# A tenth of a softmax's exponentials moved from ScalarE to VectorE, and the score banks of PSUM split 3+2+1

## The chip, the core and the metric

The kernel runs on one core of a Trainium2 chip. Its engines work side by side, each through its own queue in order: TensorE (PE in the profile; PEld is its weight load), VectorE (DVE), ScalarE (ACT), GpSimd (POOL), and SyncE (SP), which issues the DMAs. TensorE writes its results into PSUM, which has eight banks of 128 partitions by 512 fp32 numbers; VectorE and ScalarE read them from there. The metric is the time of one execution on the device in microseconds (us), the median of several.

## The reference

One token sequence of 2048 rows and 512 columns goes through a layer normalisation, and its result through two branches that are added to the input:

```python
xn = layernorm(x)                                  # 2048 x 512
q, k, v = split(xn @ wqkv)                         # 32 heads of 16
p = softmax(q @ k.T * 16**-0.5)                    # per head 2048 x 2048
A = (p @ v).reshape(2048, 512) @ wo
B = (relu(xn @ W_gate) * (xn @ W_up)) @ W_down     # 1792 wide
out = x + A + B                                    # bf16
```

The softmax needs 32 x 2048 x 2048 exponentials. With a head size of only 16, they are far more work than the matmuls per head would suggest.

## The kernel before

**Tiles.** Scores are computed transposed: a score tile is 128 keys by 512 queries of one head, fp32, one PSUM bank. There are 2048 of them, in the order of the list `tiles` (line 554): block of queries `c4` (4), group of heads `gg` (4), half `ee` (2), key tile `kt` (16), head `j` of four (the four heads sit in four strips of 32 partitions). Three tiles at a time make a unit (`UNIT = 3`, lines 555 and 751), 683 units in all, the last with two tiles. For each unit TensorE writes three score tiles into one half of `ps_sc` (six banks: two halves of three; line 765), ScalarE reads the three banks with one instruction, takes exp(x/4) and writes bf16 into a `ring` of 13 units (line 777). For each four tiles of one key tile TensorE multiplies the exponentials by `v_aug` (four small matmuls in four column strips, line 737) and accumulates over the 16 key tiles in bank 0 of `ps_b`. `v_aug` has a column of ones beside the 16 of v, so the sum of the exponentials comes along as a 17th row.

**After 16 key tiles** `normalise` (line 703) has VectorE copy bank 0 to `o_sb`, sends the row sums through two small DMAs with a reciprocal on VectorE between them, brings them back spread over the partitions (`rb`), and GpSimd multiplies (line 723).

**Everything else goes into bank 1 of `ps_b`**, the only free bank: the projections q and k, the gated branch (`glu`, line 593: four matmuls for `up`, a VectorE copy, four for `gate`, and a VectorE instruction for relu times up, line 612), and the output rows (`out_rows`, line 623: 14 matmuls with `Wd` and 8 with `Wo_p`, and an addition on VectorE). This work is cut into pairs of matmuls; a plan (lines 665 to 698) gives each pair a unit at which it is due.

**What sets the order.** The kernel records its operations with a duration each (`G.op`), and a planner (`Graph.run`) puts them into one fixed queue per engine by these durations, by priorities and by which buffers come free. Score matmuls have the best priority, and the exponentials' multiplication with v comes `PV_LAG` units later. `Graph.emit` then writes the queues with semaphore waits. On the chip nothing is reordered: an instruction that waits holds up all that stands behind it on its engine.

**Fillers.** In a unit in which no pair is due (from unit 25 on), TensorE runs two matmuls of zeros into the score bank ahead of the scores (line 763); their result is overwritten. There are 418 such matmuls.

Of the kernel before, what the change touches and what calls it, by code (L numbers as in the profile page):

```python
# [7 lines left out]
I32 = mybir.dt.int32  # L8
ACTF = mybir.ActivationFunctionType
# [16 lines left out]
UNIT = 3  # L26
NRING = 13
PV_LAG = 4.0
NWS = 4
NUP = 2  # L30
# [26 lines left out]
class Graph:  # L57
# [10 lines left out]
    def op(self, eng, dur, fn, reads=(), writes=(), prio=0.0, order=(), name="", stream=None, lat=None, after=None):  # L68
# [13 lines left out]
        for t in writes:  # L82
# [21 lines left out]
    def run(self):  # L104
# [46 lines left out]
        while n < len(ops):  # L151
# [18 lines left out]
            for t in o.acq:  # L170
                i = slot_for(t)[1]
                c = t.pool.cur[i]
                if c is not None:
                    for u in c.w + c.r:
                        if u.eng == e and e != "SP":
# [121 lines left out]
def bass_parallel_sum__mha_block__glu_gated_reglu__prompt_kernel(  # L297
# [14 lines left out]
    with ExitStack() as es:  # L312
# [24 lines left out]
        qT = sb("qT", [128, 6, 512], BF16)  # L337
        v_aug = sb("v_aug", [128, NT, H, VW], BF16)
        ring = sb("ring", [128, NRING * UNIT, 512], BF16)
# [6 lines left out]
        oT2 = sb("oT2", [128, 6, 512], BF16)  # L346
# [6 lines left out]
        P_b = Pool("b", 2)  # L353
        P_ring = Pool("ring", NRING)
        P_xn = Pool("xn", 4)
        P_q = Pool("q", 6)
# [5 lines left out]
        P_oT = Pool("oT", 14)  # L362
# [78 lines left out]
        def ln_block(b, pr):  # L441
# [24 lines left out]
            for i in range(4):  # L466
# [8 lines left out]
                elif i % 2 == 0:  # L475
                    tp = Tile("tp", P_b, [0, 1] if b < 3 else [1])
# [57 lines left out]
        def proj_k(gg, b, prio=0.0, tile=None, sub=0, slots=None, gap=0.02):  # L534
            t = tile or Tile("pk", P_b, [0, 1] if (gg, b) in ((0, 1), (0, 2)) else [1])
# [19 lines left out]
        units = [tiles[i:i + UNIT] for i in range(0, len(tiles), UNIT)]  # L555
        NU = len(units)

        def upos(c4, gg=0, ee=0, kt=0):
            return (((c4 * NGG + gg) * 2 + ee) * NT + kt) * 4 / UNIT
# [18 lines left out]
        for kt in range(NT):  # L578
            proj_v(kt, -684 + 10 * (kt // 4) + 0.1 * kt, allowed=(0, 1) if kt < 8 else (1,))


# [144 lines left out]
        def pv_group(key, kt, u):  # L726
# [6 lines left out]
            def pv(e):  # L733
                ins = None
                for j in range(4):
                    tr, i = src[j]
                    ins = e.matmul(ps_b[32 * j:32 * j + VN, 0, :], v_aug[:, kt, 8 * gg + 2 * j + ee, 0:VN],  # L737
                                   ring[:, UNIT * tr.slot + i, :], start=(kt == 0), stop=(kt == NT - 1), tile_position=(0, 32 * j))
                return ins
            rd = [t_vones, t_v[kt]]  # L740
            for tr, i in src:
# [8 lines left out]
        li = 0  # L750
        for u, cl in enumerate(units):
# [3 lines left out]
            ts = Tile("s%d" % u, P_sc)  # L755
            n = len(cl)

            def sc(e, ts=ts, cl=cl, idle=u > 24 and u not in busy):
                ins = None
                if idle:  # L760

                    for _ in range(2):
                        e.matmul(ps_sc[:, 3 * ts.slot, :], zeros[:, 0:128], zeros[:], start=True, stop=True)  # L763
# [56 lines left out]
```

## Time and profile before

| what | value |
| --- | --- |
| median of 3 runs | 969.16 us (968.02 to 971.45) |
| the profiled execution | 971.93 us, of which the span of its instructions 970.0 us |
| busy ACT | 925.9 us, 95% |
| busy PE | 804.9 us, 83% |
| busy DVE | 192.6 us, 20% |
| busy POOL | 54.0 us, 6% |
| DMA | 34.64 MB moved |
| granted TensorE clock, mean | 0.98 of full speed |

Lines such as L777 are lines of the kernel before. In the views by group, a row has the line, the engine, the operation, what it writes and reads, shapes and count; then busy time in us and the mean duration of one in ns; then the engine's idle time just ahead of them and what ended it. In the views by order of time, a row has its start in us from the start of the span and its length; equal instructions that follow each other are merged, so that a length can cover several. A duration in the profile runs from an instruction's start to its end. Instructions of one engine overlap there, since the next one starts while the last is draining; so the step from one to the next is shorter than the duration, and it is the step that counts when an engine is full.

### The profile page before, as it was taken

The page shows a single profiled execution, that of the slowest core. Times are in us where ns is not written, and L with a number is a line of the kernel's source. Part 1 is how long each engine was busy: PE and PEld are TensorE (multiplying, and loading weights), DVE is VectorE, ACT ScalarE, POOL GpSimd, SP SyncE. Part 2 cuts the span into 40 slices and gives each one's busy share as a digit, 9 for nine tenths or more (in the row PEclk, how much of TensorE's full clock was granted, in tenths as well). Part 3 has the DMA queues.
Part 4 walks back from the last instruction along what each step waited for, and adds up shares of the span by engine and source line. Part 5 has one row for each costly group of instructions (what it writes and reads, how often), then busy time and mean ns, then how long its engine had stood idle before and what let it go on. Part 6 is the DMA issues. An engine that isn't in the chain of part 4 may idle for free.

```text
span 970.0 us, 12635 instructions
## 1 busy us (share of the span) xinstructions
PE 804.9 (83%) x5482; PEld 205.6 (21%) x5584; DVE 192.6 (20%) x323; ACT 925.9 (95%) x690; POOL 54.0 (6%) x56
## 2 busy tenths in 40 slices
PE   7798888888888888888888888888888888888883
PEld 2222222222222222222222222222222222222220
DVE  7733122221000021111100111121100002221021
ACT  4699999999999999999999999999999999999992
POOL 3200000000000000000000000000000000000000
PEclk8899999999999999999999999999999999999996
DMA  5014011110000121111000011111100112210000
GB/s 159 16 41 108 18 33 34 34 34 12 2 28 29 39 50 29 23 39 45 12 23 23 26 30 46 45 45 30 26 2 23 35 34 70 57 40 22 23 13 33
DMA packets 84087, 34.64 MB, mean 36 GB/s; under 512 B 69952, under 2 KB 79936, under 8 KB 84032
## 3 DMA queue, kind: packets, MB, share of 16 engines
q1 hardware_dynamic: 84032, 33.83, 13.5%
q8 instruction: 44, 0.72, 0.3%
q14 instruction: 11, 0.09, 0.0%
HBM read 31.20 MB, written 2.36 MB: 35 GB/s over the span
## 4 chain that ended last, share of the span: by engine, by line
ACT 82%; PE 12%; DVE 3%; DMA 1%; issue 1%; SPq 0%; POOLq 0%; ACTq 0%
ACT ring L777 82%; PE ps_b L518 4%; PE ps_sc L763 3%; PE ps_sc L765 3%; PE ps_b L737 2%; DVE kT L542 1%; DMA x_sb<-in_A_x_dram 1%; DVE xn_sb L469 1%; DMA rb<-rec_scr 0%; PE ps_sc L518 0%; DVE v_aug L550 0%; DVE stats L456 0%; PE ps_b L486 0%; DVE xn_sb L648 0%; DMA rsum<-o_sb 0%
## 5 line engine op out<-in xcount | busy, mean ns | idle before, releaser
L777 ACT ACTIVATE ring<-ps_sc 128x1536 bf16<-128x1536 f32 (+1 forms) x683 | 921.5, 1655 | 15.6 <-PE ps_sc L765 13.8
L765 PE MATMUL ps_sc<-qT,kT 32*128 32x512 bf16 x2048 | 268.0, 387 | 96.1 <-ACT ring L777 70.9
L737 PE MATMUL ps_b<-ring,v_aug 128*17 128x512 bf16 x2048 | 202.0, 388 | 2.9 <-DVE o_sb L708 1.8
L763 PE MATMUL ps_sc<-zeros 128*128 128x512 bf16 x398 | 122.1, 384 | 25.1 <-ACT ring L777 16.3
L765 PEld LDWEIGHTS ps_sc<-qT,kT 32*128 32x128 bf16 x2048 | 66.2, 91 | 351.9 <-ACT ring L777 253.7
L737 PEld LDWEIGHTS ps_b<-ring,v_aug 128*17 128x17 bf16 x2048 | 49.2, 88 | 169.4 <-issue 159.2
L608 DVE COPY up_sb<-ps_b 128x512 f32<-128x512 f32 x56 | 38.7, 692 | 206.2 <-PE ps_b L518 206.2
L518 PE MATMUL ps_b<-xnT,wgs 128*128 128x512 bf16 x211 | 65.3, 386 | 2.5 <-issue 2.0
L518 PE MATMUL ps_b<-xnT,wus 128*128 128x512 bf16 x198 | 62.4, 389 | 5.7 <-issue 3.8
L518 PE MATMUL ps_b<-Wd,hT 128*128 128x512 bf16 x206 | 63.7, 384 | 2.7 <-issue 2.5
L612 DVE SCALAR_TENSOR_TENSOR hT<-ps_b,up_sb 128x512 bf16<-128x512 f32 x56 | 38.7, 692 | 122.7 <-PE ps_b L518 122.7
L723 POOL TENSOR_TENSOR x_sb<-o_sb,rb 128x512 bf16<-128x512 f32 x20 | 25.4, 1270 | 549.2 <-DMA rb<-rec_scr 520.1
L708 DVE COPY o_sb<-ps_b 128x512 f32<-128x512 f32 x32 | 22.1, 690 | 133.9 <-PE ps_b L737 133.9
L763 PEld LDWEIGHTS ps_sc<-zeros 128*128 128x128 bf16 x418 | 24.6, 97 | 88.4 <-ACT ring L777 79.8
L648 DVE TENSOR_TENSOR xn_sb<-ps_b,xr_sb 128x512 bf16<-128x512 f32 x12 | 8.3, 692 | 146.9 <-PE ps_b L518 146.9
L723 POOL TENSOR_TENSOR oT<-o_sb,rb 128x512 bf16<-128x512 f32 x12 | 15.2, 1269 | 334.2 <-DMA rb<-rec_scr 334.2
L542 DVE TENSOR_SCALAR kT<-ps_b,hmask 128x512 bf16<-128x512 f32 x32 | 22.6, 746 | 26.6 <-PE ps_b L518 26.5
L518 PE MATMUL ps_b<-Wo_p,x_sb 128*128 128x512 bf16 x70 | 22.4, 387 | 1.1 <-issue 1.1
L518 PE MATMUL ps_b<-xnT,Wk 128*128 128x512 bf16 x60 | 18.9, 407 | 1.9 <-DVE kT L542 1.1
L518 PEld LDWEIGHTS ps_b<-xnT,wus 128*128 128x128 bf16 x224 | 13.0, 97 | 27.5 <-issue 23.1
L518 PE MATMUL ps_b<-Wv,xnT 128*128 128x512 bf16 x61 | 17.1, 388 | 1.7 <-DVE xnT L500 0.9
L518 PEld LDWEIGHTS ps_b<-xnT,wgs 128*128 128x128 bf16 x224 | 12.7, 97 | 26.7 <-issue 22.9
(51 smaller groups left out, 172.0 us busy)
## 6 DMA issues: line engine op xcount, KB each, us to landing
rb<-rec_scr SPq DMA_DIRECT2D x32, 256.0 KB
wus<-in_B_W_up_dram SPq DMA_DIRECT2D x56, 128.0 KB, 2.6
wgs<-in_B_W_gate_dram SPq DMA_DIRECT2D x56, 128.0 KB, 2.3
xr_sb<-in_A_x_dram SPq DMA_DIRECT2D x16, 128.0 KB, 4.6
out_dram<-xn_sb SPq DMA_DIRECT2D x16, 128.0 KB, 1.7
Wd<-in_B_W_down_dram SPq DMA_DIRECT2D x1, 1792.0 KB, 9.9
x_sb<-in_A_x_dram SPq DMA_DIRECT2D x3, 512.0 KB, 4.0
Wv<-in_A_wqkv_dram SPq DMA_DIRECT2D x1, 512.0 KB, 7.4
```

The source lines that it names most:

```text
L469: G.op("DVE", 360, lambda e, m=m, t=t_n: e.tensor_scalar(xn_sb[:, t.slot, :], xs(m), mv[:, m, 0:1], rstd[:, m:m + 1], op0=ALU.subtract, op ...
L518: ins = e.matmul(bank_of(tile, sub), l(), r(), start=(i == 0), stop=(i == n - 1))
L542: G.op("DVE", 690, lambda e, ee=ee: e.tensor_scalar(dsts[ee], bank_of(t, sub), hmask[:, ee:ee + 1], None, op0=ALU.mult), reads=[t, t_masks ...
L608: G.op("DVE", 690, lambda e: e.tensor_copy(up_sb[:, tup.slot, :], bank_of(tu)), reads=[tu], writes=[tup], prio=slots[1])
L612: G.op("DVE", 690, lambda e: e.scalar_tensor_tensor(out=hT[:, FT * th.slot + ft, :], in0=bank_of(tg), scalar=0.0, in1=up_sb[:, tup.slot, : ...
L648: G.op("DVE", 690, lambda e: e.tensor_tensor(xn_sb[:, to_.slot, :], bank_of(t, sub), xr_sb[:, txr.slot, :] if first else resid(i), ALU.add ...
L708: G.op("DVE", 690, lambda e: e.tensor_copy(o_sb[:, to.slot, :], ps_b[:, 0, :]), reads=[tp], writes=[to], prio=-950, name="oev%d" % n)
L723: G.op("POOL", 1200, lambda e: e.tensor_tensor(oT_of(tn), o_sb[:, to.slot, :], rb[:, trb.slot, :], ALU.mult), reads=[to, trb], writes=[tn] ...
L737: ins = e.matmul(ps_b[32 * j:32 * j + VN, 0, :], v_aug[:, kt, 8 * gg + 2 * j + ee, 0:VN], ring[:, UNIT * tr.slot + i, :], start=(kt == 0), ...
L763: e.matmul(ps_sc[:, 3 * ts.slot, :], zeros[:, 0:128], zeros[:], start=True, stop=True)
L765: ins = e.matmul(ps_sc[:, 3 * ts.slot + i, :], kT[32 * j:32 * j + 32, 2 * gg + ee, 128 * kt:128 * kt + 128], qT[32 * j:32 * j + 32, t_q[(c ...
L777: return e.activation(ring[:, UNIT * tr.slot:UNIT * tr.slot + n, :], ps_sc[:, 3 * ts.slot:3 * ts.slot + n, :], ACTF.Exp, scale=0.25)
```

## The change

**Exponentials on VectorE.** Of the 2048 score tiles, spread evenly over the tiles 96 to 2007, 208 are taken out of the units, two after two. For each, TensorE writes the scores into a third bank of `ps_b`, used for nothing else, and VectorE makes fixed-point numbers of them (`d1`: scale by 0.25 log2(e) 65536, clamp, int32 out). Then, for two tiles together, 1024 elements per partition: the low 16 bits of each number are the fraction f, the high 16 bits the whole part n. Three instructions (`d2`, `d3`, `d4`) evaluate a cubic for 2^f in factored form, bf16 out, and a fourth (`d5`) adds 128 n to the bits of that bf16 as an integer, which puts n into the exponent. The result goes into a ring of three pairs, `dring`, and the multiplication with v reads it from there. `d2` writes into the space of the weights `Wv`, which are no longer needed by then.

**Score banks 3+2+1.** `ps_sc` has five banks in place of six: units have three tiles and two tiles by turns, each kind in banks of its own and in a ring of its own (seven of each). `ps_b` has three banks in place of two. Before VectorE's first tile, the start of the kernel may use the third for projections.

**What goes along.** `PV_LAG` is 7 in place of 4. A unit without a due pair gets one filler matmul in place of two (261 in all). To make room, `qT` has 4 buffers in place of 6, the gated branch 3 pairs of weight buffers in place of 4 and one `up_sb` in place of two, and `oT2` 2 in place of 6. Two rules of the planner change: on VectorE and GpSimd, an instruction that overwrites what an earlier one of the same engine read now waits for it.

```diff
-UNIT = 3
-NRING = 13
-PV_LAG = 4.0
-NWS = 4
-NUP = 2
+SIZES = (3, 2)
+NRING = 7
+PV_LAG = 7.0
+NWS = 3
+NDR = 3
+ND_TILES = 210
+D_FIRST = 96
+D_LAST = 2048 - 40
...
+NUP = 1
...
-                if r.eng == eng and eng != "SP":
+                if r.eng == eng and eng in ("PE", "ACT"):
                     o.order.add(r)
...
-        ps_sc = es.enter_context(nc.psum_tensor("ps_sc", [128, 6, 512], FP32))
-        ps_b = es.enter_context(nc.psum_tensor("ps_b", [128, 2, 512], FP32))
+        ps_sc = es.enter_context(nc.psum_tensor("ps_sc", [128, 5, 512], FP32))
+        ps_b = es.enter_context(nc.psum_tensor("ps_b", [128, 3, 512], FP32))
...
+            ts = Tile("ds", P_b, [2])
+            G.op("PE", 300, lambda e: score(e, ps_b[:, 2, :], t), reads=[t_q[t[:2]], t_k[(t[1], t[2], t[3] // 4)]], writes=[ts],
+                 prio=u - 2000, order=[last_d[0]] if last_d else [], name="dsc")
...
+            G.op("DVE", 700, lambda e: e.tensor_scalar(dt_sb[:, td.slot, 512 * i:512 * i + 512], ps_b[:, 2, :], 0.25 * LOG2E * FX, -127.0 * FX,
+                                                       op0=ALU.mult, op1=ALU.max), reads=[ts], writes=[td], prio=u - 4, name="d1")
+            if i == 0:
+                return
...
+            def half(k):
+                return dt_sb[:, td.slot, :].bitcast(I16 if k else U16)[:, k::2]
+            tv, tq, tw = Tile("dv", P_dv), Tile("dq", P_dq), Tile("dw", P_dw)
+            G.op("DVE", 600, lambda e: e.tensor_scalar(Wv[:, :, :].rearrange("p a b -> p (a b)").bitcast(FP32), half(0), C_C * FX, C_K / FX ** 3, op0=ALU.add, op1=ALU.mult),
+                 reads=[td], writes=[tv], prio=u - 3, name="d2")
+            G.op("DVE", 1140, lambda e: e.scalar_tensor_tensor(out=dq_sb[:], in0=half(0), scalar=C_A * FX, in1=half(0), op0=ALU.add, op1=ALU.mult),
+                 reads=[td], writes=[tq], prio=u - 3, name="d3")
+            G.op("DVE", 1140, lambda e: e.scalar_tensor_tensor(out=dw_sb[:], in0=dq_sb[:], scalar=C_B * FX * FX, in1=Wv[:, :, :].rearrange("p a b -> p (a b)").bitcast(FP32),
+                                                               op0=ALU.add, op1=ALU.mult),
+                 reads=[tq, tv], writes=[tw], prio=u - 3, name="d4")
+            G.op("DVE", 1140, lambda e: e.scalar_tensor_tensor(out=dring[:, tr.slot, :].bitcast(I16), in0=half(1), scalar=128.0,
+                                                               in1=dw_sb[:].bitcast(I16), op0=ALU.mult, op1=ALU.add),
+                 reads=[td, tw], writes=[tr], prio=u - 3, name="d5")
...
-            ts = Tile("s%d" % u, P_sc)
+            k0 = u % 2
+            ts = Tile("s%d" % u, P_sc, [k0])
             n = len(cl)
...
-                    for _ in range(2):
-                        e.matmul(ps_sc[:, 3 * ts.slot, :], zeros[:, 0:128], zeros[:], start=True, stop=True)
...
+                    e.matmul(ps_sc[:, 3 * k0, :], zeros[:, 0:128], zeros[:], start=True, stop=True)
...
+            def ex(e, tr=tr, n=n, k0=k0):
+                a = 3 * tr.slot if k0 == 0 else 3 * NRING + 2 * tr.slot
+                return e.activation(ring[:, a:a + n, :], ps_sc[:, 3 * k0:3 * k0 + n, :], ACTF.Exp, scale=0.25)
```

The numbers in `G.op` (700, 600, 1140) are what the planner takes for a duration. In the changed kernel the lines are L796 for the scores, L777 for the multiplication with v, L848 for the fillers, L865 for the exponentials on ScalarE, L537 for pairs of matmuls, and L810, L821, L823, L825 and L828 for `d1` to `d5`.

**How the queues are moved.** The first place is TensorE's queue where a block's output rows are accumulated (pairs with `Wd`). Before, with three score tiles (L765) in each unit:

```order
L765 MATMUL ps_sc<-qT,kT 128x512 x3
L518 MATMUL ps_b<-Wd,hT 128x512 x2
L737 MATMUL ps_b<-ring,v_aug 17x512 x4
L765 MATMUL ps_sc<-qT,kT 128x512 x3
L518 MATMUL ps_b<-Wd,hT 128x512 x2
L737 MATMUL ps_b<-ring,v_aug 17x512 x4
L765 MATMUL ps_sc<-qT,kT 128x512 x3
```

And now:

```order
L796 MATMUL ps_sc<-qT,kT 128x512 x3
L537 MATMUL ps_b<-Wd,hT 128x512 x2
L796 MATMUL ps_sc<-qT,kT 128x512 x2
L796 MATMUL ps_b<-qT,kT 128x512
L537 MATMUL ps_b<-Wd,hT 128x512 x2
L777 MATMUL ps_b<-ring,v_aug 17x512 x4
L796 MATMUL ps_sc<-qT,kT 128x512 x3
L537 MATMUL ps_b<-Wd,hT 128x512 x2
L796 MATMUL ps_sc<-qT,kT 128x512 x2
```

Units of three and of two tiles follow each other, each still with its pair. The single score matmul into `ps_b` is that of a VectorE tile, and it stands in the same queue as all else.

The second place is VectorE's queue in the middle of the kernel. Before, it only empties banks for the gated branch (L608, L612), the attention sums (L708, L716) and the projections:

```order
L608 COPY up_sb<-ps_b 128x512
L612 SCALAR_TENSOR_TENSOR hT<-ps_b,up_sb 128x512
L708 COPY o_sb<-ps_b 128x512
L716 RECIPROCAL rrec<-rsum 128x16
L608 COPY up_sb<-ps_b 128x512
```

And now:

```order
L823 SCALAR_TENSOR_TENSOR dq_sb<-dt_sb 128x1024
L653 SCALAR_TENSOR_TENSOR hT<-ps_b,up_sb 128x512
L825 SCALAR_TENSOR_TENSOR dw_sb<-dq_sb,Wv 128x1024
L749 COPY o_sb<-ps_b 128x512
L828 SCALAR_TENSOR_TENSOR dring<-dt_sb,dw_sb 128x1024
L810 TENSOR_SCALAR dt_sb<-ps_b 128x512
L757 RECIPROCAL rrec<-rsum 128x16
L810 TENSOR_SCALAR dt_sb<-ps_b 128x512
L821 TENSOR_SCALAR Wv<-dt_sb 128x1024
```

The same copies and products that free a bank (L653, L749) now stand between the long instructions of the exponentials.

More of the change, by code (lines that the diff above doesn't have):

```diff
@@ L8 @@
 I32 = mybir.dt.int32
+I16 = mybir.dt.int16
+U16 = mybir.dt.uint16
 ACTF = mybir.ActivationFunctionType
@@ L754, in bass_parallel_sum__mha_block__glu_gated_reglu__prompt_kernel, with sc @@
                 li += 1
[L755 removed]
+            k0 = u % 2
+            ts = Tile("s%d" % u, P_sc, [k0])
             n = len(cl)
[L758 removed]
+            while tiles[ti] != cl[-1]:
+                if ti in on_dve:
+                    dve_exp(tiles[ti], u)
+                ti += 1
+            def sc(e, cl=cl, k0=k0, idle=u > 24 and u not in busy):
                 ins = None
                 if idle:
[L762 to L766 removed]
+                    e.matmul(ps_sc[:, 3 * k0, :], zeros[:, 0:128], zeros[:], start=True, stop=True)
+                for i, t in enumerate(cl):
+                    ins = score(e, ps_sc[:, 3 * k0 + i, :], t)
                 return ins
```

97 lines of the change are left out of this document (71 added, 26 removed).

## The prediction

> **What bounds the kernel now.** I read the page first: busy time and the chain of waits.
>
> ```profile
> span 970.0 us, 12635 instructions
> ...
> PE 804.9 (83%) x5482; PEld 205.6 (21%) x5584; DVE 192.6 (20%) x323; ACT 925.9 (95%) x690; POOL 54.0 (6%) x56
> ...
> ACT 82%; PE 12%; DVE 3%; DMA 1%; issue 1%; SPq 0%; POOLq 0%; ACTq 0%
> ```
>
> ScalarE is busy for 95% of the span and carries 82% of the chain; TensorE is the only other large share. Next, the chain in order of time gives the step from one exponential to the next, where ScalarE never waits:
>
> ```profile
> 598.58 6.83 ACT ring L777 x5
> ...
> 800.70 150.62 ACT ring L777 x112
> 951.33 0.93 ACTq L275
> ...
> 952.29 0.42 PE ps_b L737 x4
> ...
> 966.67 0.69 DVE xn_sb L648
> ```
>
> 112 instructions on three banks take 150.62 us: 1.345 us each. The piece of 0.93 is the kernel's only exponential on two banks, the last unit; the exponential ahead ends at 951.33, and the next piece of work starts at 952.29, 0.05 after what releases it (below), so its step is 0.91 to 0.92. I take 0.916. The durations in the groups are longer than these steps, because neighbours overlap:
>
> ```profile
> L777 ACT ACTIVATE ring<-ps_sc 128x1536 bf16<-128x1536 f32 x682 | 920.6, 1656 | 15.6 <-PE ps_sc L765 13.8
> ...
> L777 ACT ACTIVATE ring<-ps_sc 128x1024 bf16<-128x1024 f32 x1 | 1.1, 1067 | 0.0
> ```
>
> So all exponentials need 682 x 1.345 + 0.916 = 918.2 us. The rest of the span comes from a table by stages (length, then busy us of PE, PEld, DVE, ACT and POOL, clock, DMA):
>
> ```profile
> 0.00:17.60 17.60, 12.60 (x48) 4.87 (x48) 11.68 (x30) 4.36 (x7) 7.32 (x19) 0.81 0.59 179
> 17.60:60.00 42.40, 33.92 (x236) 11.55 (x238) 29.04 (x53) 33.15 (x25) 6.02 (x5) 0.92 0.10 26
> 60.00:130.00 70.00, 61.05 (x436) 15.93 (x444) 20.94 (x32) 69.41 (x52) 3.80 (x3) 1.00 0.28 68
> 130.00:200.00 70.00, 58.95 (x399) 14.74 (x402) 16.45 (x25) 68.84 (x52) 2.54 (x2) 0.98 0.10 25
> ...
> 600.00:700.00 100.00, 83.68 (x575) 20.93 (x586) 18.02 (x29) 99.23 (x75) 3.82 (x3) 0.98 0.14 33
> ...
> 800.00:900.00 100.00, 84.94 (x585) 21.00 (x594) 25.22 (x40) 99.93 (x76) 3.81 (x3) 1.00 0.19 46
> ...
> 952.30:970.00 17.70, 2.64 (x8) 0.43 (x8) 3.61 (x6) 0.00 (x0) 1.26 (x1) 0.58 0.14 45
> ```
>
> Head 17.6 us before the first exponential; 42.4 - 33.15 = 9.25 us idle while the first blocks are projected; tail 17.7 us after the last one. 17.6 + 918.2 + 9.25 + 17.7 = 962.8. The 7.2 us that are missing to 970.0 were lost between exponentials after 60 us: late scores.
>
> **The change, part by part.**
>
> *ScalarE.* The order now has 368 exponentials on three banks and 368 on two: 368 x (1.345 + 0.916) = 832.0 us. That takes 86.2 us off the engine that sets the end. The two-bank step rests on one instruction; if it were 0.90 (two thirds of 1.345, no fixed cost at all) the sum would be 6 us less, and it can't be much more, since 0.92 was seen.
>
> *TensorE.* The steps between neighbouring instructions, from two stretches in order of time:
>
> ```profile
> 504.00 1.65 ACT L777 ACTIVATE ring<-ps_sc 128x1536 bf16<-128x1536 f32 x1
> ...
> 505.70 0.39 PE L765 MATMUL ps_sc<-qT,kT 32*128 32x512 bf16 x3
> ...
> 506.03 0.60 PE L518 MATMUL ps_b<-Wd,hT 128*128 128x512 bf16 x2
> ...
> 506.56 0.39 PE L737 MATMUL ps_b<-ring,v_aug 128*17 128x512 bf16 x4
> ...
> 597.60 0.61 PE L763 MATMUL ps_sc<-zeros 128*128 128x512 bf16 x2
> ...
> 598.14 0.39 PE L765 MATMUL ps_sc<-qT,kT 32*128 32x512 bf16 x3
> ...
> 598.46 0.39 PE L737 MATMUL ps_b<-ring,v_aug 128*17 128x512 bf16 x4
> ...
> 598.79 0.60 PE L763 MATMUL ps_sc<-zeros 128*128 128x512 bf16 x2
> ```
>
> A unit's scores take 0.325 us, a pair 0.53, four matmuls with v 0.32, two fillers 0.54, one filler 0.54 - 0.22 = 0.32 (two matmuls last 0.60, one 0.39). A VectorE tile's single score matmul is bounded by zero (beside scores of other strips it can run along) and by the 0.33 of a group; I take 0.31, since it mostly stands alone in the order. By the counts of the orders TensorE's work was 222 (scores) + 164 (v) + 263 (pairs) + 112 (fillers) = 761 us, 83% of 918; now it is 239 + 164 + 259 + 64 (new scores) + 81 = 807 us, 97% of 832. I added these prices along both orders and summed what exceeds ScalarE's time in a stretch. Before: 3.7 us with stretches of four units, 17.3 with two; the trace lost 7.2, a quarter of the way between. After: 28.5 and 40.7; at the same place that is **31 us** lost. The lower bound is stretches of ten, 9.7 us; the overfull ones are where pairs stand in every unit (output rows).
>
> *The split of the banks* makes this sharper. An exponential that ends at 505.65 releases its banks, and the next scores start 0.05 later (505.70); they last 0.39, and the exponential starts 0.05 after them (598.14 + 0.39, then 598.58). An exponential alone lasts 1.45 us:
>
> ```profile
> 42.11 1.45 ACT L777 ACTIVATE ring<-ps_sc 128x1536 bf16<-128x1536 f32 x1 [2.43 <-PE ps_sc L765]
> ```
>
> Before, the next exponential in the same banks had to end 2 x 1.345 = 2.69 us later, so scores could start 2.69 - 1.45 - 0.44 = 0.80 us after the release. Now the two ends are 2.26 apart: 0.37 for the three-bank half, and 0.80 again for the two-bank half (an exponential alone is 0.43 shorter there). One filler (0.32) just fits into 0.37; a pair in progress does not. I leave this inside the 31.
>
> *VectorE.* The rows nearest to the new operations, the last of them from the chain:
>
> ```profile
> L608 DVE COPY up_sb<-ps_b 128x512 f32<-128x512 f32 x56 | 38.7, 692 | 206.2 <-PE ps_b L518 206.2
> L612 DVE SCALAR_TENSOR_TENSOR hT<-ps_b,up_sb 128x512 bf16<-128x512 f32 x56 | 38.7, 692 | 122.7 <-PE ps_b L518 122.7
> ...
> L457 DVE BATCH_NORM_AGGREGATE mv<-stats 128x2 f32<-128x6 f32 x16 | 2.6, 172 | 0.0
> ...
> L723 POOL TENSOR_TENSOR x_sb<-o_sb,rb 128x512 bf16<-128x512 f32 x20 | 25.4, 1270 | 549.2 <-DMA rb<-rec_scr 520.1
> ...
> 28.56 1.28 DVE xn_sb L469 x4
> ```
>
> `d1`, like L608, reads one bank: 0.69 us, twice per pair of tiles. `d2` is a TENSOR_SCALAR from SBUF to SBUF; the nearest row is L469, 1.28 / 4 = 0.32 per 512 elements, so 0.64; the upper bound is the slope below, 1.23. `d3` to `d5` read two operands of SBUF on VectorE, which no row shows. L612 has one from PSUM: with about 0.16 fixed (L457, hardly any elements, has 0.17) its slope is (0.692 - 0.16) / 512 = 1.04 ns per element, and 1024 elements take 0.16 + 1.06 = 1.23 us. Bounds: twice L469's rate, 0.64, and GpSimd's L723, which does read two operands of SBUF, 2 x 1.27 = 2.54. I take 1.23, as L612 is the same operation on the same engine. `d4` waits for `d3` and `d5` for `d4`, so whole durations count. A pair of tiles: 2 x 0.69 + 0.64 + 3 x 1.23 = 5.71 us; 104 pairs: 594 us. VectorE's other work after 60 us and before the tail is 192.6 - 11.7 - 29.0 - 3.6 = 148 us. Together 742 of some 836 us: 89%.
>
> A page of the Trainium skill has two statements on this price. Vector Engine (DVE) Microarchitecture Reference, "Measured stream behaviour on trn2", gives built-in two-source operations one element per cycle, 1.04 ns, and about 75 ns per instruction; by it an estimate for the three is 1.14 us each, and for the pair 5.4; L612's slope agrees. "Points that are easy to get wrong" on the same page says that this very operation runs at half throughput with two sources in SBUF that are not bf16; no row here shows it, and it is a rival below.
>
> A pair of VectorE tiles comes with 1912 / 104 - 2 = 16.4 tiles on ScalarE, 7.41 us. The stretch of 800 to 900 us becomes 91 us with 12.2 pairs, 69.8 + 25.2 = 95.0 us of VectorE: 4 over. 60 to 130 becomes 63.4 with 48.9 + 20.9: 6 over; 130 to 200, 2 over; 600 to 700 fits (69.8 + 18.0). Some of these 12 us fall where TensorE is overfull as well: I count **8**.
>
> *At no cost:* fewer buffers for weights, queries and `oT` (their loads and copies are ordered units ahead), `PV_LAG` (a longer lag, with 14 units of ring as before 13), the new waits on VectorE for its own reads (inside the full durations). Head, first blocks and tail keep their work; with less cover the buffers would show as DMA waits of TensorE, some 2 us for each weight that comes late.
>
> *Sum:* 17.6 + 832.0 + 9.3 + 31 + 8 + 17.7 = 915.6 us of span; the profiled execution has 971.93 for a span of 970.0, so 917.5; and the median of the runs is 2.8 below that execution: **915 us**.
>
> **The rivals.**
>
> *Hand-offs cost no more than now.* For it: every stretch of twenty units but a few fits TensorE. Against it: 97% of work, and 0.37 in place of 0.80 us. With 7 us lost and none for VectorE: 17.6 + 832 + 9.3 + 7 + 17.7 + 1.9 - 2.8 = 883 us.
>
> *TensorE waits for VectorE.* All 208 new scores go through one bank that VectorE must have read; that read stands behind instructions of 1.23 us, and whatever waits at TensorE holds up the scores for ScalarE. So do the gate matmuls, which wait for the copy of `up`, and v's, which wait for `d5`. For it: VectorE at 89% and TensorE with no slack left. Against it: the order gives other work between. If a third of the 208 wait for half such an instruction, 0.6 us, that is 42 us more: 957. It becomes a loss beyond 55 us, where some 90 of the 208 wait so long.
>
> *The three long instructions run at half rate.* With 2.08 ns per element each takes 2.3 us, near GpSimd's 2.54; a pair takes 8.9 and all 926, with the other work 1074 us. With 60 ahead and about 34 behind the last one, that is a span of 1168. This ends on the other side; it decides from (970 - 60 - 34 - 148) / 104 = 7.0 us per pair, that is (7.0 - 2.0) / 3 = 1.66 us for each of the three. For it, the trace has only that GpSimd row and the unseen pair of operands; against it, L612's slope. The Trainium skill's second statement above would make it so.
>
> That it doesn't do what it says I exclude: the order has 208 tiles out of ScalarE's instructions.
>
> **How the numbers follow.** Forecast (895 to 935): 0.55. Hand-offs free (below 895): 0.10. TensorE behind VectorE (935 to 966): 0.18; beyond it, up to just over 1000: 0.04. Half rate (about 1170): 0.13. The range leaves out half rate, the worst coupling and an edge: 887 to 957. What this kernel's measurement can tell from no change is about 0.3%, 3 us. Faster takes the first two cases and nearly all of the third, 0.82; same 0.02; slower 0.16.
>
> **What would show it.** Exponentials 368 + 368 with steps of 1.35 and 0.92: ScalarE's part. ScalarE's idle time after 60 us should be about 40 us, ended by score matmuls; less, and the first rival holds. TensorE's waits for VectorE's `d1` (L810) should be some us in total; tens would be the second rival. The mean of L823, L825 and L828 should be near 1230 ns; 2.3 us means the third. A wait of TensorE for weights, or of ScalarE for its ring, would show a buffer that I took as free. Wrong altogether would be a step on two banks that grows under the new load, for which nothing in the profile speaks.

## The result, and the profile after

The changed kernel takes **903.55 us** (median of 3 runs, 903.36 to 904.14), against 969.16 us before: 0.932 of the time (95% interval 0.929 to 0.935). That is 65.6 us less; 54 were forecast.

The page of the changed kernel, busy time and the chain of waits:

```profile
span 901.3 us, 13005 instructions
...
PE 794.2 (88%) x5328; PEld 220.4 (24%) x5427; DVE 741.8 (82%) x947; ACT 845.9 (94%) x743; POOL 62.7 (7%) x56
...
ACT 56%; PE 30%; DVE 8%; DMA 2%; issue 1%; POOL 0%; SPq 0%; POOLq 0%; ACTq 0%
```

ScalarE lost 80 us of work and is still busy for 94% of the span, but its share of the chain fell from 82% to 56%, and TensorE's rose from 12% to 30%: the two now hand the bound to and fro. The table by stages (length, then busy us of PE, PEld, DVE, ACT and POOL, clock, DMA) cuts the span at the first exponential, at 60 us and behind the last exponential:

```profile
0.00:15.90 15.90, 11.14 (x51) 4.45 (x51) 11.84 (x30) 4.36 (x7) 7.31 (x19) 0.89 0.64 198
15.90:60.00 44.10, 39.80 (x266) 13.45 (x270) 36.85 (x64) 34.74 (x31) 6.01 (x5) 0.96 0.22 66
60.00:883.70 823.70, 740.58 (x5012) 202.03 (x5098) 689.50 (x848) 806.76 (x706) 48.11 (x31) 0.99 0.13 34
883.70:901.30 17.60, 2.65 (x8) 0.44 (x8) 3.62 (x6) 0.00 (x0) 1.26 (x1) 0.54 0.14 46
```

Head 15.9 us, 44.1 - 34.7 = 9.4 idle in the first blocks, tail 17.6. With 832.0 us of exponentials that makes 874.9, so 26.4 us were lost between exponentials after 60 us, against 7.2 before. Idle time proper is less, because a late exponential also loses its overlap with the one ahead of it: 823.7 - 806.8 = 16.9 us of ScalarE after 60 us, where the kernel before has 3.9:

```profile
60.00:952.30 892.30, 755.77 (x5197) 188.73 (x5295) 148.29 (x235) 888.39 (x659) 39.36 (x31) 0.99 0.13 33
```

The groups by shape show the exponentials and VectorE's new work:

```profile
L865 ACT ACTIVATE ring<-ps_sc 128x1536 bf16<-128x1536 f32 x368 | 545.5, 1482 | 21.2 <-PE ps_sc L796 19.6
L865 ACT ACTIVATE ring<-ps_sc 128x1024 bf16<-128x1024 f32 x368 | 389.3, 1058 | 7.8 <-PE ps_sc L796 7.2 <-PE ps_b L796 0.4
...
L810 DVE TENSOR_SCALAR dt_sb<-ps_b 128x512 int32<-128x512 f32 x208 | 142.1, 683 | 20.9 <-PE ps_b L796 16.1 <-PE ps_sc L796 4.4
L823 DVE SCALAR_TENSOR_TENSOR dq_sb<-dt_sb 128x1024 f32<-128x1024 uint16 x104 | 130.6, 1255 | 0.0
L828 DVE SCALAR_TENSOR_TENSOR dring<-dt_sb,dw_sb 128x1024 int16<-128x1024 int16 x104 | 129.3, 1243 | 9.5 <-PE ps_b L777 9.3
L825 DVE SCALAR_TENSOR_TENSOR dw_sb<-dq_sb,Wv 128x1024 bf16<-128x1024 f32 x104 | 128.9, 1239 | 0.3
...
L821 DVE TENSOR_SCALAR Wv<-dt_sb 128x1024 f32<-128x1024 uint16 x104 | 72.2, 694 | 1.5
```

ScalarE's waits are for scores, and nearly three quarters of them stand ahead of three-bank units (21.2 of 29.0 us over the whole span). `d3` to `d5` take 1.24 to 1.26 us, `d1` 0.68, `d2` 0.69. In the chain, the longest stretch in which ScalarE runs through, and the kernel's end:

```profile
686.84 75.04 ACT ring L865 x66
...
882.75 0.92 ACTq L289
```

66 exponentials by turns on three and two banks take 75.04 us, 2.274 for two, where 1.345 + 0.916 = 2.261 was reckoned; the last two-bank step is 0.92 again.

### The profile page after: what moved, and what is told of

It is laid out like the page before. It is cut to its first block, busy times and chain, and to the rows that moved or that the text cites. A ratio compares the mean times of both kernels' runs of the same rounds, so it can differ in the third digit from the quotient of the medians.

```text
span 901.3 us, 13005 instructions
## 1 busy us (share of the span) xinstructions
PE 794.2 (88%) x5328; PEld 220.4 (24%) x5427; DVE 741.8 (82%) x947; ACT 845.9 (94%) x743; POOL 62.7 (7%) x56
## 4 chain that ended last, share of the span: by engine, by line
ACT 56%; PE 30%; DVE 8%; DMA 2%; issue 1%; POOL 0%; SPq 0%; POOLq 0%; ACTq 0%
ACT ring L865 56%; PE ps_b L537 11%; PE ps_sc L796 9%; PE ps_b L777 5%; PE ps_sc L848 3%; PE ps_b L796 2%; DVE dq_sb L823 2%; DMA rb<-rec_scr 1%; DVE dt_sb L810 1%; DVE Wv L821 1%; DVE xn_sb L488 1%; DVE dw_sb L825 1%; DMA x_sb<-in_A_x_dram 1%; DVE dring L828 1%; DVE v_aug L569 0%
## 5 line engine op out<-in xcount | busy, mean ns | idle before, releaser
L865 ACT ACTIVATE ring<-ps_sc 128x1536 bf16<-128x1536 f32 x736 | 841.5, 1270 | 29.0 <-PE ps_sc L796 26.8
L796 PE MATMUL ps_sc<-qT,kT 32*128 32x512 bf16 x1840 | 291.8, 388 | 43.9 <-ACT ring L865 36.2
L777 PE MATMUL ps_b<-ring,v_aug 128*17 128x512 bf16 x1840 | 192.4, 385 | 3.5 <-DVE o_sb L749 1.5
L810 DVE TENSOR_SCALAR dt_sb<-ps_b 128x512 int32<-128x512 f32 x208 | 142.1, 683 | 20.9 <-PE ps_b L796 16.1
L828 DVE SCALAR_TENSOR_TENSOR dring<-dt_sb,dw_sb 128x1024 int16<-128x1024 int16 x104 | 129.3, 1243 | 9.5 <-PE ps_b L777 9.3
L796 PEld LDWEIGHTS ps_sc<-qT,kT 32*128 32x128 bf16 x1840 | 70.3, 91 | 258.5 <-ACT ring L865 163.9
L823 DVE SCALAR_TENSOR_TENSOR dq_sb<-dt_sb 128x1024 f32<-128x1024 uint16 x104 | 130.6, 1255 | 0.0
L825 DVE SCALAR_TENSOR_TENSOR dw_sb<-dq_sb,Wv 128x1024 bf16<-128x1024 f32 x104 | 128.9, 1239 | 0.3
L848 PE MATMUL ps_sc<-zeros 128*128 128x512 bf16 x235 | 90.9, 387 | 17.7 <-ACT ring L865 16.8
L796 PE MATMUL ps_b<-qT,kT 32*128 32x512 bf16 x208 | 80.3, 386 | 3.2 <-DVE dt_sb L810 1.8
L777 PE MATMUL ps_b<-dring,v_aug 128*17 128x512 bf16 x208 | 80.1, 385 | 0.0
L777 PEld LDWEIGHTS ps_b<-ring,v_aug 128*17 128x17 bf16 x1840 | 45.4, 88 | 126.2 <-issue 118.1
L821 DVE TENSOR_SCALAR Wv<-dt_sb 128x1024 f32<-128x1024 uint16 x104 | 72.2, 694 | 1.5
L537 PE MATMUL ps_b<-Wd,hT 128*128 128x512 bf16 x209 | 65.8, 402 | 3.9 <-issue 2.6
L537 PE MATMUL ps_b<-xnT,wgs 128*128 128x512 bf16 x216 | 61.5, 383 | 4.2 <-DVE up_sb L649 2.8
L537 PE MATMUL ps_b<-xnT,wus 128*128 128x512 bf16 x197 | 61.1, 390 | 4.4 <-issue 4.1
L653 DVE SCALAR_TENSOR_TENSOR hT<-ps_b,up_sb 128x512 bf16<-128x512 f32 x56 | 38.4, 686 | 12.8 <-PE ps_b L537 12.3
L848 PEld LDWEIGHTS ps_sc<-zeros 128*128 128x128 bf16 x261 | 25.1, 96 | 86.5 <-ACT ring L865 70.9
L649 DVE COPY up_sb<-ps_b 128x512 f32<-128x512 f32 x56 | 38.3, 684 | 5.1 <-PE ps_b L537 4.8
L749 DVE COPY o_sb<-ps_b 128x512 f32<-128x512 f32 x32 | 22.0, 688 | 15.8 <-PE ps_b L777 15.7
L537 PE MATMUL ps_b<-Wo_p,x_sb 128*128 128x512 bf16 x101 | 31.9, 386 | 1.6 <-issue 1.1
```

What stands on the lines that cost most here:

```text
L537: ins = e.matmul(bank_of(tile, sub), l(), r(), start=(i == 0), stop=(i == n - 1))
L653: G.op("DVE", 690, lambda e: e.scalar_tensor_tensor(out=hT[:, FT * th.slot + ft, :], in0=bank_of(tg), scalar=0.0, in1=up_sb[:, tup.slot, : ...
L796: return e.matmul(bank, kT[32 * j:32 * j + 32, 2 * gg + ee, 128 * kt:128 * kt + 128], qT[32 * j:32 * j + 32, t_q[(c4, gg)].slot, :], start ...
L810: G.op("DVE", 700, lambda e: e.tensor_scalar(dt_sb[:, td.slot, 512 * i:512 * i + 512], ps_b[:, 2, :], 0.25 * LOG2E * FX, -127.0 * FX, op0= ...
L821: G.op("DVE", 600, lambda e: e.tensor_scalar(Wv[:, :, :].rearrange("p a b -> p (a b)").bitcast(FP32), half(0), C_C * FX, C_K / FX ** 3, op ...
L823: G.op("DVE", 1140, lambda e: e.scalar_tensor_tensor(out=dq_sb[:], in0=half(0), scalar=C_A * FX, in1=half(0), op0=ALU.add, op1=ALU.mult), ...
```

## The experiments

Two measures run through all of them, both read from the traces between 60 us and the tail. *Late* is, summed over the exponentials, the time from the end of one to the end of the next beyond the next one's step (1.345 or 0.916 us). *Half clock* is the time for which the trace has TensorE's granted clock at one half; it is only ever 1 or one half. "Three-bank, filler" is the late time of three-bank units whose scores have a filler right ahead and run at full clock; "at half clock" is that of units whose scores run at half clock. The sums were reckoned from the instructions of each trace.

```
run                     time us  half clock  late  of it: three-bank, filler  at half clock
kernel before             969.2        10 us   6.1                       5.8            0.0
changed kernel            903.6        20     25.6                      14.5            6.5
no filler                 945.7       280     66.6                       -             57.0
split only               1034.6       150     57.9                      13.7           38.9
d3, d4 on 64 columns      903.0        27     27.1                      14.0            9.3
VectorE +0.98 us a pair   971.6       126    102.8                      35.1           40.8
two fillers               942.4        14     64.8                      49.5            5.4
before, one filler        981.4       150     18.2                       4.4           13.5
split only, two fillers  1028.0         3     51.2                      47.0            0.4
fillers in two-bank       910.6        58     38.0                       -             18.7
short fillers             902.1        17     23.5                      10.6            7.1
228 tiles                 910.5        38     38.2                      18.7           12.4
178 tiles                 928.0        44     39.0                      15.4           13.0
```

(Before, all units but the last have three banks. Times are medians; late and half clock are of the profiled execution, which is a single one. Where it lies more than 4 us from the median, small differences of these columns say little: 980.9 us with more work for VectorE, 917.5 with fillers in two-bank units, 905.7 with 228 tiles and 934.0 with 178.)

### No filler at all

```diff
-                if idle:
-                    e.matmul(ps_sc[:, 3 * k0, :], zeros[:, 0:128], zeros[:], start=True, stop=True)
```

> The changed kernel without its 261 filler matmuls; every queue else stands as it was. Theory (the time lost between exponentials after 60 us, about 25 us in the profile of the changed kernel, is TensorE at 97% of ScalarE's time): TensorE's work falls from 807 to about 726 us, 87%, and the loss to 12 us or less, so 888 to 894 us. Rival (the fillers keep TensorE's clock up, and are worth what they cost): the granted clock falls below 0.95 in some stretches, score matmuls get longer, and the time is 903 us or more.

945.7 us, 0.973 of the kernel before (0.967 to 0.978), 42 us above the changed kernel: the rival held, and the theory, which had the fillers as a cost alone, was wrong. Of the 66.6 us late, 57.0 fall on units at half clock. Two stretches of 100 us:

```profile
660.00:760.00 100.00, 94.30 (x514) 18.72 (x512) 71.68 (x85) 89.40 (x78) 5.46 (x4) 0.70 0.09 25
760.00:860.00 100.00, 94.35 (x655) 25.79 (x654) 96.96 (x124) 100.00 (x89) 6.32 (x4) 1.00 0.22 54
```

TensorE looks equally busy in both, but in the first it ran at a mean clock of 0.70, did 514 matmuls in place of 655, and ScalarE stood idle for 10.6 us; in the second, at full clock and without a filler, it lost nothing. A filler costs TensorE 0.32 us (the prediction's step) and yet is worth more than it costs here, because without any the clock is at half for 280 us in place of 20. At half clock a unit's scores take longer:

```profile
246.53 0.61 PE L796 MATMUL ps_sc<-qT,kT 32*128 32x512 bf16 x2
```

0.61 in place of 0.39 us. TensorE's other work takes longer with it: a multiplication with v 0.438 us on average over this run, 0.385 in the changed kernel.

### The split of the banks alone

```diff
-ND_TILES = 210
+ND_TILES = 0
```

> The score banks 3+2+1 and all else of the change, but no tile on VectorE: 410 exponentials on three banks and 409 on two. Theory (the gain is the tiles that ScalarE no longer has, and the split costs a little): 410 x 1.345 + 409 x 0.916 = 926 us of exponentials, TensorE at 86% of that, 7 to 12 us lost after 60 us, so with 16 us head, 9 us in the first blocks, 17.6 us tail and 2 us outside the span 976 to 983 us. Rival (the shorter time for the three-bank half, 0.37 us, costs at each filler and each pair that is in progress): 20 us or more lost, 990 us or above.

1034.6 us: 1.067 of the kernel before (1.061 to 1.074). The rival's bound, 990 us or above, held; its mechanism is only the smaller part. Exponentials of 926 us explain 8 of the 65 us more, and late time, 57.9 us against 6.1, nearly all of the rest. Two thirds of the late time, 38.9 us, falls on units at half clock, which neither theory had; the trace is at half clock for 150 us. The view by cores gives the mean clock:

```profile
core 0: 1031.4 us, clock 0.915
```

So with one filler and without VectorE's tiles the clock is not held, and the split suffers from it. With two fillers (below) the clock comes back and the time does not. The run also keeps the longer lag, the smaller buffers and the planner's rules; what is late neither behind a filler ahead of three banks nor at half clock is 57.9 - 13.7 - 38.9 = 5.3 us, so they have at most a small part in it.

### VectorE's part made light

```diff
+        G.op("POOL", 1200, lambda e: e.memset(dw_sb[:], 1.0), writes=[gw], prio=-400)
...
-    out=dq_sb[:], in0=half(0), ..., in1=half(0)
+    out=dq_sb[:, 0:64], in0=half(0)[:, 0:64], ..., in1=half(0)[:, 0:64]
...
-    out=dw_sb[:], in0=dq_sb[:], ..., in1=Wv...
+    out=dw_sb[:, 0:64], in0=dq_sb[:, 0:64], ..., in1=Wv...[:, 0:64]
```

> The same queues, but the second and third of the four long VectorE instructions (d3 and d4) work on 64 columns in place of 1024, so most of the polynomial is left out; VectorE has about 210 us less to do. Theory (VectorE holds up nobody for long; the loss is TensorE's own): within 4 us of the changed kernel's 903.6. Rival (part of the 25 us are waits for VectorE's banks, as my 8 us in the sum or more): 895 us or less.

(GpSimd fills `dw_sb` once at the start, so that the columns left out hold numbers.)

903.0 us (0.929 of before, 0.922 to 0.935), not to be told from the changed kernel, with 194 us less work on VectorE. Its row from 60 us to the tail, to be held against the 689.50 above:

```profile
60.00:884.00 824.00, 762.53 (x5108) 201.08 (x5105) 495.72 (x849) 805.43 (x707) 42.66 (x31) 0.98 0.13 34
```

TensorE's waits for `d1` and for the copy of `up` (L810 and L649 in the changed kernel, where they are 11.9 and 7.9 us, shown below) fall with it:

```profile
PEld ps_b L798 <- DVE dt_sb L812: 3.7, 9, 1.1
PEld ps_b L537 <- DVE up_sb L651: 3.2, 9, 0.4
```

The theory held: in the changed kernel VectorE holds nobody up for long enough to show in the time. The time alone is a weak witness, since its interval reaches from about 10 us below the changed kernel to 2 above. The late time is the stronger one: without the units at half clock it is 27.1 - 9.3 = 17.8 us here and 25.6 - 6.5 = 19.1 in the changed kernel, 1.3 us apart and not 8.

### VectorE's part made heavier

```diff
+        spare = sb("spare", [128, 304], BF16)
...
+        def extra(e, half):
+            e.scalar_tensor_tensor(out=spare[:], in0=half(0)[:, 0:304], scalar=C_A * FX, in1=half(0)[:, 0:304], op0=ALU.add, op1=ALU.mult)
...
-            G.op("DVE", 1140, lambda e: e.scalar_tensor_tensor(out=dq_sb[:], ...
+            G.op("DVE", 1140, lambda e: extra(e, half) or e.scalar_tensor_tensor(out=dq_sb[:], ...
...
-            G.op("DVE", 1140, lambda e: e.scalar_tensor_tensor(out=dw_sb[:], ...
+            G.op("DVE", 1140, lambda e: extra(e, half) or e.scalar_tensor_tensor(out=dw_sb[:], ...
```

> The same queues with two more VectorE instructions of 304 columns per pair of tiles, which write nothing that is used; about 0.45 us each, 94 us in all, which takes VectorE from 83% to about 95% of the time between 60 us and the tail. Theory (there is slack, and VectorE decides only near 100%): 903 to 915 us. Rival (TensorE waits for VectorE as soon as its queue is late, since the single bank and the gate's bank stand between them): 920 us or more.

971.6 us, 0.999 of the kernel before (0.996 to 1.002): the whole gain is gone, for about 80 us more of VectorE (769.4 us between 60 us and the tail, in place of 689.5). The rival held. Its waits:

```profile
ACT ring L869 <- PE ps_sc L797: 87.8, 140, 3.6
PEld ps_b L797 <- DVE dt_sb L814: 65.4, 113, 1.9
...
PE ps_b L797 <- DVE dt_sb L814: 26.9, 58, 1.6
PEld ps_b L538 <- DVE up_sb L650: 20.8, 40, 2.0
```

TensorE waits for `d1` (L814 here) to read the one bank of VectorE's scores, and for the copy of `up`. The same waits in the changed kernel:

```profile
PEld ps_b L796 <- DVE dt_sb L810: 11.9, 28, 1.1
PEld ps_b L537 <- DVE up_sb L649: 7.9, 18, 1.1
```

The clock falls as well: 126 us at half clock in place of 20, and a mean clock of 0.947 or less in each of the ten executions, where the changed kernel has 0.976 or more. The queues are the same and only VectorE's load is changed, so the onset of the second rival lies between 84% of VectorE's time (689.5 of 823.7 us) and some 93% (769.4 of the same).

### Two fillers

```diff
-                    e.matmul(ps_sc[:, 3 * k0, :], zeros[:, 0:128], zeros[:], start=True, stop=True)
+                    for _ in range(2):
+                        e.matmul(ps_sc[:, 3 * k0, :], zeros[:, 0:128], zeros[:], start=True, stop=True)
```

> The changed kernel with two fillers in a unit without a due pair (522 in place of 261), as the kernel before had. Theory (TensorE's work is what counts, and it is full): 807 + 57 = 864 us of work for 832 us of exponentials, so TensorE becomes the bound there, 915 to 930 us, at a clock of 0.98 or more. Rival (fillers stand only where TensorE has time, and hold the clock): 898 to 906 us.

942.4 us (0.971, 0.969 to 0.974) at a clock of 0.98: the clock is held, and the time lies above the theory's 915 to 930. 49.5 of the 64.8 us late are three-bank units behind fillers: 129 units, 0.38 us each. So not only the sum of TensorE's work counts, as the theory had it, but also where the two fillers stand, ahead of scores that have 0.37 us; the split alone with two fillers (below) shows the same.

### The kernel before with one filler

```diff
-                    for _ in range(2):
+                    for _ in range(1):
                         e.matmul(ps_sc[:, 3 * ts.slot, :], zeros[:, 0:128], zeros[:], start=True, stop=True)
```

> The kernel before with one filler in place of two in a unit without a due pair (209 in place of 418). Theory (TensorE's granted clock follows how busy it is, and the old banks leave 0.80 us, which hides slower scores): the clock falls below 0.95, but the time stays within 2% of the kernel before, 965 to 990 us. Rival A (the old fillers cost more than they give): clock as before, 960 to 968 us. Rival B (one filler breaks the old kernel as it does the split one): above 1000 us.

981.4 us, 1.010 of the kernel before (1.007 to 1.013), with as much half clock as the split alone (150 us) but only 18.2 us late. The mean clock is the same as there, and the price is a fraction:

```profile
core 0: 980.2 us, clock 0.909
```

The theory held: with 0.80 us between release and deadline, slower scores still come in time mostly. A unit at half clock is late by 0.15 us on average here (13.5 us over 89 units), and by 0.47 us in the split kernel (38.9 over 82).

### The split alone, with two fillers

The edits of the split alone and of two fillers together.

> The split of the banks without a tile on VectorE, as in the run that took 1034.6 us at a clock of 0.915, now with two fillers per unit without a due pair (688 in place of 344). Theory (what made that run slow was the clock): clock 0.97 or more, 926 us of exponentials and some 25 us lost, 985 to 1000 us. Rival (two fillers of 0.54 us do not fit into the 0.37 us of the three-bank half, whatever the clock): 1015 us or more.

1028.0 us, 1.061 of before (1.056 to 1.066), at a clock of 0.985: the rival held. 47.0 of 51.2 us late are three-bank units behind two fillers, 170 of them by 0.28 us each. The prediction's arithmetic gives nearly this size: two fillers delay scores by 0.05 + 0.54 = 0.59 us where the three-bank half allows 0.37, which is 0.22 too late. So the split costs its 60 us either way: with one filler mostly by the clock, with two by the fillers.

### Fillers where there is room

```diff
-                    e.matmul(...)
+                    for _ in range(2 * k0):
+                        e.matmul(...)
```

> The changed kernel with the same number of fillers, but two in each unit of two tiles without a due pair and none in units of three. Theory (a filler of 0.32 us uses up the 0.37 us that the three-bank half has, while the two-bank half has 0.80): the loss after 60 us falls from 25 to some 15 us, 890 to 898 us, at the same clock. Rival (the loss is not at the fillers): 900 to 907 us; or, if a gap in every other unit lets the clock fall, above 907.

910.6 us (0.940 of before, 0.935 to 0.944): the theory fell, and the rival's second branch held, with a lower clock and more than 907 us. The mean clock was 0.953 to 0.968 in its four executions. Three-bank units at full clock are now late by 15.9 us without a filler right ahead, against 14.5 + 4.0 in the changed kernel, and half clock lasts 58 us in place of 20. Taking the filler away ahead of the three-bank units did not bring them in time.

### Short fillers

```diff
-                    e.matmul(ps_sc[:, 3 * k0, :], zeros[:, 0:128], zeros[:], start=True, stop=True)
+                    for w in ((256,) if k0 == 0 else (512, 256)):
+                        e.matmul(ps_sc[:, 3 * k0, 0:w], zeros[:, 0:128], zeros[:, 0:w], start=True, stop=True)
```

> The changed kernel with the same columns of zeros, laid out otherwise: 256 ahead of the scores of a unit of three without a due pair, 512 and 256 ahead of those of a unit of two. Theory (units of three behind a filler lose 14.5 us in the changed kernel, since 0.32 us nearly uses up their 0.37): with 0.21 us they lose some 8 us less, and the clock stays: 893 to 898 us. Rival (those units are late because TensorE as a whole is, whatever stands right ahead of them, as the run with two fillers or none suggested): 901 to 911 us.

902.1 us, 0.930 of before (0.927 to 0.932), not to be told from the changed kernel (0.929 to 0.935). Three-bank units behind a filler lose 10.6 us in place of 14.5; the theory's 8 us less did not come, and the rival's 901 to 911 us held. The trace of the changed kernel says why. A unit's banks are released when the exponential two units ahead ends. Of the three-bank units at full clock, 278 start their scores within 0.40 us after that, and none of them is late by more than 0.05 us; of the 69 that start later, 67 are. Those that start 0.45 to 0.50 us after it are late by 0.11 us on average, which puts the deadline at the prediction's 0.37. One filler alone keeps it: 77 of the 128 units behind a filler start in time. The scores of the 50 that are late start 0.68 us after the release on average, and for all but 0.02 us of that TensorE is at work, on the filler and on what was in progress or stood ahead of it. A shorter filler shortens this delay and does not remove it.

### More and fewer tiles on VectorE

```diff
-ND_TILES = 210
+ND_TILES = 230        # the other run: 180
```

> 228 tiles on VectorE in place of 208, the orders made anew. Exponentials on ScalarE: 364 x 1.345 + 363 x 0.916 = 822 us, 10 less; VectorE between 60 us and the tail goes from 83 to about 91%. Theory (VectorE holds up TensorE from somewhere between 83% and the 95% that cost 68 us): 905 to 935 us, with tens of us of waits for VectorE's reading of the score bank. Rival (208 leaves room): 890 to 900 us.

910.5 us (0.938 of before, 0.935 to 0.941): 7 us slower than 208 tiles, though ScalarE has 10 us less to do. The theory held as to time; its mechanism only in small part, since TensorE's waits for `d1` grew from 11.9 to 15.4 us, not to tens:

```profile
PEld ps_b L796 <- DVE dt_sb L810: 15.4, 36, 1.2
```

The late time grew by 12.6 us, half of it at half clock.

> 178 tiles on VectorE in place of 208, the orders made anew. Exponentials on ScalarE: 374 x (1.345 + 0.916) = 845.6 us, 13.6 more. Theory (each tile that moves is worth its 0.45 us on ScalarE, the losses stay): 915 to 920 us. Rival (the score matmuls for VectorE also hold TensorE's clock up, as the run without any of them had it at half for 150 us): 922 us or more, with over 40 us at half clock.

928.0 us (0.955 of before, 0.949 to 0.961): 24 us slower for 13.6 us more of exponentials. The rival's time and its 44 us at half clock held. Its cause is shown in part: of the 13.4 us more late time, 6.5 fall on units at half clock, and the rest stays open, since the orders are others. So 208 is near the best of what was tried, from both sides; no run beat it by more than the spread of the runs.

## Why the prediction was right

The direction, the size within 12 us and the mechanism of the gain were right: 86 us less on the engine that sets the end, part of it given back in late scores. That the sum came out so near is in part luck: two terms were too large, and time at half clock, which the sum does not have, made up for some of it.

- **ScalarE, 832.0 us.** Right: the two-bank step of 0.916, read from a single instruction, held under load within 0.6% (2.274 for two steps against 2.261).
- **Head, first blocks and tail, 17.6 + 9.3 + 17.7.** Measured 15.9, 9.4 and 17.6. The head's 1.7 us were not expected; in the chain its first load takes 5.04 us in place of 6.47. Whether the third bank has a part in it stays open.
- **TensorE, 31 us, and VectorE, 8 us.** Together 39; measured 26.4. The 8 is the term that was mis-sized: with a light VectorE the late time beside half clock falls by 1.3 us only. I had used whole durations for `d3` to `d5` and called 89% of VectorE's time, and three stretches overfull; it was 84%. The durations were right (1.23 us against 1.24 to 1.26); but where another instruction stands between two dependent ones, as it does behind 202 of the 208 `d3` and `d4`, it is the step that counts, and that is 1.13 us. Two pieces of the chain show it:

```profile
680.07 1.13 DVE dq_sb L823
681.20 1.15 DVE dring L828
```

- **TensorE at 97%, interpolated between two lengths of stretch.** 31 forecast, 26.4 at most measured, or 25.6 step by step. The mechanism is the one named under the split, work in progress that does not fit into 0.37 us; the interpolation to 31 is not confirmed as such. The sum took the clock as given, and of the 25.6 us late, 6.5 are at half clock.
- **Fillers as a cost alone.** This was the real gap. The prediction had 81 us of fillers in TensorE's sum (261 at its 0.32 us are 83.5) and nothing for what they buy. Without them the kernel takes 945.7 us, with twice as many 942.4, with the one per unit that the change chose 903.6. Without VectorE's tiles one filler or two can't be told apart (1.061 to 1.074 and 1.056 to 1.066).
- **The split at no price of its own.** The shorter deadline, 0.37 in place of 0.80 us, was worked out and then left "inside the 31". Its arithmetic held, unit by unit, but without VectorE's tiles the split costs 6 to 7%. With them late time at half clock is 6.5 us in place of 38.9. That their score matmuls keep TensorE busier, and so the clock up, fits this and the run with 178 tiles, but no run changes them alone.
- **The rivals.** Hand-offs free (883 us) came nearer than I allowed: the result lies 12 us under the forecast and 21 above that. TensorE waiting for VectorE is real but not here: it cost 68 us at about 93% of VectorE, and its waits for `d1`, 11.9 us, lie between the "some us" that were forecast and the tens that the rival asked for. The sign for the first rival was less than about 40 us of idle time; 16.9 came, or 26.4 as the sum counts it, so the truth lies between that rival's 7 and the forecast's 39. Half rate fell: 1.24 us, not 2.3. The Trainium skill's statement in "Points that are easy to get wrong" (Vector Engine (DVE) Microarchitecture Reference) that this operation runs at half throughput with two sources in SBUF that are not bf16 is not borne out for fp32, uint16 and int16 sources here; the step of 1.13 agrees with its "Measured stream behaviour on trn2", by which I had estimated 1.14.
- **At no cost: fewer buffers, the longer lag.** In the view of waits of the changed kernel, TensorE never waits for a DMA, and ScalarE's exponentials only for scores, so neither weights nor the ring's room held anything up. TensorE waits for products of GpSimd at the end, as before (10.8 us in both kernels), and otherwise at most 1.0 us at a time, at 683 us (below).

## What to carry to other kernels

When work leaves the bounding engine, reckon the deadline of each hand-off anew: here the time that scores may take after a bank's release fell from 0.80 to 0.37 us, and that made the kernel sensitive to things that cost nothing before. An instruction that fills TensorE is not only a cost; price it by what the clock does without it, and try the change with none, one and two. An engine that others wait for in order has no use for its last tenth: VectorE at 84% cost nothing that could be measured, and at some 93% it cost the whole gain.

## What the hardware showed

**The clock halves without a long pause.** In the changed kernel the longest stretch at half clock begins at 253.5 us. Stretches of 3.41 us, the unit in which it starts and ends:

```profile
246.68:250.09 3.41, 3.00 (x21) 0.88 (x21) 3.38 (x7) 3.41 (x4) 0.00 (x0) 1.00 0.21 45
250.09:253.50 3.41, 2.26 (x18) 0.57 (x18) 3.31 (x5) 3.41 (x4) 0.00 (x0) 1.00 0.33 116
253.50:263.74 10.24, 9.52 (x33) 2.05 (x35) 8.59 (x10) 7.13 (x7) 1.27 (x1) 0.50 0.00 0
263.74:267.15 3.41, 3.41 (x24) 0.81 (x23) 1.71 (x3) 3.16 (x3) 0.00 (x0) 1.00 0.00 0
```

The clock is full while TensorE is busy for 2.26 of 3.41 us, with no pause longer than 1 us, and then half for three such units, in which ScalarE loses 3.1 us. I counted each matmul with the 0.216 us by which it delays the next (four in a row last 1.04 us and one 0.39), and matmuls that run along each other once. By that count TensorE was at work for 0.17 to 0.56 of the 3.41 us ahead of each of the 118 halvings between 60 us and the tail in the thirteen traces. Below a share of 0.40, 42 stretches were followed by half clock and 2 were not; from 0.40 to 0.45, 42 and 20; from 0.45 to 0.50, 25 and 86; from 0.50 to 0.60, 9 and 659; above, none of 2146. So the edge is soft and lies near 0.45 of such a stretch. What exactly is counted stays open, and some matmul records are missing from the traces.

**VectorE and GpSimd hold each other up.** At the same place `d3`, which reads two operands in SBUF, takes twice its time, when a multiplication on GpSimd started just ahead of it:

```profile
253.62 1.27 POOL L764 TENSOR_TENSOR x_sb<-o_sb,rb 128x512 bf16<-128x512 f32 x1 [26.14 <-DMA rb<-rec_scr]
253.68 2.29 DVE L823 SCALAR_TENSOR_TENSOR dq_sb<-dt_sb 128x1024 f32<-128x1024 uint16 x1
```

2.29 us in place of 1.22. GpSimd's instruction ends at 254.89 and `d3` at 255.97, 1.08 us later, which is nearly all of its usual time: VectorE waits until GpSimd is done. It goes the other way as well: GpSimd's 28 multiplications into `x_sb` take 1.54 us on average in place of 1.27, some up to 2.37. Thirteen of VectorE's 312 long instructions are held up so, 9.5 us in all; each of the thirteen overlaps such a multiplication. The run with a light VectorE, in which `d3` and `d4` are short, is not faster by more than its spread, so most of this is covered. The Trainium skill has this rule (SBUF — State Buffer, "Who interferes with whom": a VectorE instruction with two inputs in SBUF contends with a GpSimd instruction that reads SBUF), and the trace agrees. At 682.4 us `d4` and GpSimd meet again, and TensorE's next output rows wait for GpSimd's product:

```profile
683.67 1.03 PE L537 MATMUL ps_b<-Wd,hT 128*128 128x512 bf16 x2 [0.74 <-POOL x_sb L764]
```

That wait is not a result of the meeting: GpSimd's instruction takes its usual 1.27 us there. It could not start before the last small DMA of `normalise`, issued at 677.16, whose semaphore it waited for until 682.24.
